# A causal head-wise convolution ahead of a channel mix: all of it on the path with x as the stationary operand, output with channels on partitions, and no intermediate in DRAM

## The chip, the cores and the metric

The kernel runs on one core of a Trainium2 chip. A core has a TensorE (PE) for matrix products, a VectorE (DVE), a ScalarE (ACT) and a GpSimd (POOL) for everything elementwise, a SyncE (SP) that issues DMAs here, and 16 DMA engines. The metric is the device time of one execution in microseconds (us), taken as the median of several runs. TensorE takes a *stationary* operand, loaded by an instruction of its own (LDWEIGHTS), and streams a *moving* operand past it. The array can be addressed in smaller tiles: a row "64*128" in the profile is a stationary operand of 64 partitions by 128 columns, "128*32" one of 128 partitions by 32 columns, "32*32" one of 32 by 32. Results go to PSUM[...].

## What is computed

```python
def _attn_ref(x, weight):                       # x (8, 4160, 192), weight (8, 7)
    w = softmax(weight, axis=-1)
    x_pad = concat([zeros((B, 6, D)), x], axis=1)
    idx = np.arange(S)[:, None] + np.arange(K)[None, :]
    x_unf = x_pad[:, idx, :].reshape(B, S, K, H, group)      # group = 24 channels
    return np.einsum('hk,bskhg->bshg', w, x_unf).reshape(B, S, D)

def _moe_ref(x, mu_k, mu_r, w_k, w_v, w_r):     # x is the result above; d_ff = 1024
    x_prev = x shifted by one token
    xk = mu_k * x + (1.0 - mu_k) * x_prev
    xr = mu_r * x + (1.0 - mu_r) * x_prev
    k = np.maximum(xk @ w_k, 0.0)
    v = k * k @ w_v
    r = 1.0 / (1.0 + np.exp(-(xr @ w_r)))
    return r * v
```

Each of the 8 heads filters its 24 channels along the tokens with 7 taps; then the channel mix follows.

## The kernel before

**Tiling.** The 8 batches are taken in four pairs. A pair's 4160 tokens are cut into steps of 512. The convolution's result for a pair lies in `yT`, with channels on partitions: three chunks of 64 channels, the two batches of the pair on the lower and upper 64 partitions. From it VectorE makes `diff`, `xk` and `xr` of each step.

**Bundles.** Work is issued in an order written out by hand, in 65 *bundles*. A steady bundle (`bundle_rest`) has four slots of the k product (`k_mm`, 6 matmuls of 64x512 each), four `k_relu` on ScalarE, four `k_square` on VectorE, a quad of the r product with its sigmoid (`r`, `r_out`), and a quad of the v product in two halves (`v_rows`, 32 matmuls of 64x192 each) with the multiplication `v_out`, whose result SyncE writes to `out`. The order on TensorE is k0, k1, k2, r, v half 0, k3, then the convolution's units of this bundle, then v half 1. Tables (`early`, `mix_a`, `mix_b`, `mix_c`, `late`, `xt`) say what else is issued in which bundle and at which point; `xt[b]` is the list of convolution units of bundle b. Every PSUM tile has two banks and comes from `ring`, which holds four of them; a tile is free again when the last reader is through, so a late reader on ScalarE or VectorE can hold up TensorE.

**The convolution, four ways.** `toe` holds for each head a banded matrix of taps, 128 by 128. A block is 120 new tokens with 6 of halo.

- `conv_t` (groups 0 to 2, the first 11 blocks of pair 0): x is stationary, 128 tokens by up to 32 channels; the band of a head (128x120) moves. The output has channels on partitions, and one copy (`to_yT`) per chunk puts it into `yT`. A strip of 32 channels meets two heads, so each strip takes two matmuls, the second of 24, 16 or 8 columns over the first. A block of one chunk is 8 matmuls: 2 batches, 2 strips, 2 heads.
- `conv_mm` (group 3): the band is stationary in 64x128 tiles, x moves, tokens come out on partitions; `conv_out` casts on ScalarE into `y`, and `tr` transposes on TensorE.
- `conv_tiles` (groups 4 and 5): 64x64 tiles of the band, x moves; ScalarE casts into `y` (`cast_tiles`); `y_write` sends `y` to a DRAM buffer, and `y_read` brings it back with a transposing DMA into `yT`, both from SyncE's queue.
- `conv_sparse` (groups 6 to 11, that is pairs 1 to 3): 32x32 tiles of the band, 26 new tokens of each 32 rows; 32 matmuls of 32x240, two PSUM tiles and four casts in a unit; then through DRAM as above. There are 24 such units, one in a bundle, in bundles 7 to about 51.

x comes from DRAM by DMAs that GpSimd issues and that cast to bf16 (`load_x`); small memsets on VectorE (L111, L123) order them behind the reuse of their buffers.

Of the kernel before, what the change touches and what calls it, by code (L numbers as in the profile page):

```python
# [14 lines left out]
def kernel(  # L15
# [23 lines left out]
    GB = 10  # L39
    HB = 56  # L40
    TB = 26
    TG = 20
    NROW = -(-S // (2 * HB)) * 2 * HB
# [9 lines left out]
    const = ctx.enter_context(tc.tile_pool(name="const", bufs=1))  # L53
    two = ctx.enter_context(tc.tile_pool(name="two", bufs=2))
# [3 lines left out]
    dram = ctx.enter_context(tc.tile_pool(name="dram", bufs=1, space=bass.MemoryType.DRAM))  # L58
# [32 lines left out]
    for p in range(NPAIR):  # L91
        base = 0
        for nb, s, on_pe in (
            ((3, 0, True), (4, 1, True), (4, 2, True), (5, 3, True), (10, 4, False), (10, 6, False))
            if p == 0
            else ((TG, 0, None), (TG, 4, None))
        ):
            if on_pe is None:
                base = min(base, S - nb * 4 * TB)
            groups.append((p, base, nb, first_bundle[first_step[p] + s], on_pe))  # L100
            base += nb * (4 * TB if on_pe is None else BLK if on_pe else 2 * HB)
        assert S <= base <= NROW
    sparse = {g for g, grp in enumerate(groups) if grp[4] is None}
    ends = [nxt[1] if nxt[0] == grp[0] else S for grp, nxt in zip(groups, groups[1:] + [(NPAIR,)])]


    xbs, homes = {}, {}

    def tie_x(g, s):

        nc.vector.memset(xbs[g][0:1, 1, s, 0:2], 0.0)  # L111

    def x_tile(g):
        p, base, nb, _, on_pe = groups[g]
        first = g if g in sparse else 4 * (g > 3)
        if g == first:
            homes[g] = two.tile([P, TG, 2, D], BF16, tag="xb", name="xb")
        n0 = sum(grp[2] for grp in groups[first:g])
        xb = homes[first][:, n0 : n0 + nb, :, :]
        xbs[g] = xb  # L120
        if g > 4:

            nc.vector.memset(xb[0:1, 0, 0, 0:2], 0.0)  # L123
        if base == 0 and g > 0:
            nc.gpsimd.memset(xb[0:32, 0, :, :], 0.0)  # L125
        if on_pe is False and base + 2 * nb * HB > S:
            n0 = nb - (base + 2 * nb * HB - S) // HB - 1
            nc.gpsimd.memset(xb[Q:P, n0:nb, :, :], 0.0)

    def load_x(g, batches=range(2)):  # L130
        p, base, nb, _, on_pe = groups[g]
        xb = xbs[g]
        if on_pe:
            parts, step, rows = ((0, base),), BLK, P
        elif g in sparse:
            parts, step, rows = [(32 * i, base + i * nb * TB) for i in range(4)], TB, 32
        else:
            parts, step, rows = ((0, base), (Q, base + nb * HB)), HB, Q
        for s in batches:
            b = 2 * p + s  # L140
            for q0, start in parts:
                lo, hi = 0, nb
                t0 = start - HALO
                if t0 < 0:
                    lo = 1
                    nc.gpsimd.dma_start(out=xb[HALO:rows, 0, s, :], in_=x[b, 0 : rows - HALO, :])
                while t0 + (hi - 1) * step + HALO + step > S:
                    hi -= 1
                    r0 = t0 + hi * step
                    if r0 + HALO < S:  # L150
                        nc.gpsimd.dma_start(out=xb[q0 : q0 + S - r0, hi, s, :], in_=x[b, r0:S, :])
                nc.gpsimd.dma_start(  # L152
                    out=xb[q0 : q0 + rows, lo:hi, s, :],
                    in_=bass.AP(
                        tensor=x.tensor,
                        offset=x.offset + (b * S + t0 + lo * step) * D,
                        ap=[[D, rows], [step * D, hi - lo], [1, D]],
                    ),
                )
# [140 lines left out]
    ys, yTs, y_drams = {}, {}, {}  # L300
    conv_ps = {}

    def conv_tiles(g, c):

        nb = groups[g][2]
        if c == 0:
            ys[g] = two.tile([P, GB, 2 * D], BF16, tag="y", name="y")
        ps = ring.tile([P, 2, BANK], FP32, tag="k", name="ps_c")
        conv_ps[g, c] = ps
        m = nb // 2  # L310
        banks = ps[:, :, 0 : m * 4 * G].rearrange("p i (m s c) -> p i m s c", m=m, s=2)
        for k in range(2):
            h = 2 * c + k
            for i in range(2):
                q = slice(i * Q, (i + 1) * Q)
                for j in range(2):
                    nc.tensor.matmul(  # L317
                        out=banks[j * Q : (j + 1) * Q, i, :, :, k * G : (k + 1) * G],
                        lhsT=toe[q, h, q],
                        rhs=xbs[g][q, j * m : (j + 1) * m, :, h * G : (h + 1) * G],  # L320
                        start=True,
                        stop=True,
                    )

    def conv_tiles_out(g, c):

        cast_tiles(ys[g], conv_ps.pop((g, c)), groups[g][2] // 2, c)

    def cast_tiles(y, ps, m, c):

        c0, c1 = 2 * c * G, 2 * (c + 1) * G
        cuts = [c0] + [a for a in range(Q, D, Q) if c0 < a < c1] + [c1]
        for a, b in zip(cuts, cuts[1:]):
            d = a // Q * 2 * Q + a % Q
            nc.scalar.copy(  # L335
                out=bass.AP(
                    tensor=y.tensor,
                    offset=y.offset + d,
                    ap=[y.ap[0], [m * 2 * D, 2], [2 * D, m], [Q, 2], [1, b - a]],
                ),  # L340
                in_=bass.AP(
                    tensor=ps.tensor,
                    offset=ps.offset + a - c0,
                    ap=[ps.ap[0], [BANK, 2], [4 * G, m], [2 * G, 2], [1, b - a]],
                ),
            )

    def conv_sparse(g, c):

        nb = groups[g][2]  # L350
        m = nb // 4
        if c == 0:
            ys[g] = [two.tile([P, GB, 2 * D], BF16, tag="y", name="y") for _ in range(2)]
        tiles = [ring.tile([P, 2, BANK], FP32, tag="k", name="ps_c") for _ in range(2)]
        xb = xbs[g].rearrange("p (m j) s c -> p j m s c", j=4)
        for k in range(2):
            h = 2 * c + k
            for i in range(4):
                q = slice(32 * i, 32 * i + 32)
                banks = tiles[i // 2][:, i % 2, 0 : m * 4 * G].rearrange("p (m s c) -> p m s c", m=m, s=2)  # L360
                for j in range(4):
                    nc.tensor.matmul(  # L362
                        out=banks[32 * j : 32 * j + 32, :, :, k * G : (k + 1) * G],
                        lhsT=toe[q, h, q],
                        rhs=xb[q, j, :, :, h * G : (h + 1) * G],
                        start=True,
                        stop=True,
                    )
        for y, ps in zip(ys[g], tiles):
            cast_tiles(y, ps, m, c)  # L370

    def conv_units(g):

        return [((0, 1), (6, 7)), ((2, 3), (4, 5))]

    def conv_mm(g, c, half):

        nb = groups[g][2]
        if half == 0:
            if c == 0:  # L380
                ys[g] = two.tile([P, GB, 2 * D], BF16, tag="y", name="y")
            conv_ps[g, c] = ring.tile([P, 2, BANK], FP32, tag="k", name="ps_c")
        unit = conv_units(g)[c]
        last = len(unit[0]) - 1
        banks = conv_ps[g, c][:, :, 0 : nb * 2 * G * (last + 1)].rearrange("p i (n s c) -> p i n s c", n=nb, s=2)
        for k in range(last + 1):
            for i in range(2):
                q = slice(i * Q, (i + 1) * Q)
                bank = (i + half) % 2
                h = unit[bank][k]  # L390
                nc.tensor.matmul(
                    out=banks[:, bank, :, :, k * G : (k + 1) * G],
                    lhsT=toe[q, h, :],
                    rhs=xbs[g][q, :nb, :, h * G : (h + 1) * G],
                    start=half == 0 and k == 0,
                    stop=half == 1 and k == last,
                )
        if half == 0:
            nc.scalar.clobber_nop([nc.scalar.lower_ap(conv_ps[g, c])])
# [54 lines left out]


    def y_write(g):
        p, base, nb, _, _ = groups[g]
        if base == 0:
            new_yT(p)
        if g in sparse:  # L460
# [604 lines left out]
```

## Time and profile before

Three runs took 410.29, 411.07 and 411.44 us. The profiled execution took 411.28 us; its span, from the first to the last instruction, is 409.5 us, so 1.78 us lie around it. The granted TensorE clock was 1.00.

| stretch of the span (us) | PE busy | DVE busy | ACT busy | POOL busy | mean of DMA share | GB/s |
|---|---|---|---|---|---|---|
| 0 to 12 | 9.51 | 7.42 | 7.41 | 10.38 | 0.97 | 152 |
| 12 to 28.8 | 15.47 | 15.23 | 15.76 | 7.02 | 1.59 | 190 |
| 28.8 to 57.93 | 28.95 | 27.66 | 27.37 | 6.59 | 1.24 | 217 |
| 57.93 to 312 | 253.56 | 235.45 | 231.65 | 32.23 | 0.90 | 175 |
| 312 to 409.5 | 93.74 | 84.65 | 72.46 | 0.61 | 0.39 | 108 |

The stretches are: start, ramp, the `conv_tiles` units, the `conv_sparse` units (57.93 is the first of them, 312 lies just behind the last), and the rest, in which no convolution is left. Busy times are in us; the DMA share is the busy time of the 16 DMA engines over the stretch and can exceed 1 where transfers overlap on one engine. To read it: compare each engine's busy time with the length of its stretch, then see which engine has no gap left.

### The profile page before, as it was taken

Reading aid. Unit: us, or ns where it says so; the run is one execution under the profiler, and the core shown is the slowest. Engines: PE = TensorE matmul, PEld = TensorE weight load, DVE = VectorE, ACT = ScalarE, POOL = GpSimd, SP = SyncE. Lnnn points to the kernel's source line nnn. Section 1 sums busy time; section 2 is a strip of 40 time slices with the busy share of each in tenths; the row PEclk is TensorE's granted clock in tenths of the full one; section 3 lists DMA queues with packets and bytes.
Section 4 is the critical chain, followed back from the end, with each engine's and each line's share of the span. In section 5 each row is a group of like instructions: output and inputs, shape, how many; then the busy total and the mean of one; then the engine's idle time right before and its main releaser. Section 6 shows DMA issues by size and latency. Waiting matters only on the chain.

```text
span 409.5 us, 17547 instructions
## 1 busy us (share of the span) xinstructions
PE 401.2 (98%) x7736; PEld 302.2 (74%) x7736; DVE 370.4 (90%) x672; ACT 354.6 (87%) x426; POOL 56.8 (14%) x91
## 2 busy tenths in 40 slices
PE   8899999999999999999999999999999999999996
PEld 5567777777877767777776777777777778777795
DVE  5999898988999989999999999999999899999973
ACT  6899989989888989988898998889899878877781
POOL 8622202200230202004020022000000000000000
PEclk9999999999999999999999999999999999999999
DMA  9999999997399998789995996977623856221223
GB/s 148 188 201 207 197 204 192 213 249 179 90 203 264 193 193 134 158 212 178 205 141 151 236 170 132 171 176 206 121 91 89 209 135 157 80 71 48 80 80 115
DMA packets 138955, 66.23 MB, mean 162 GB/s; under 512 B 89356, under 2 KB 138880, under 8 KB 138880
## 3 DMA queue, kind: packets, MB, share of 16 engines
q1 hardware_dynamic: 95536, 48.20, 46.9%
q0 software_dynamic: 42544, 16.36, 34.8%
q8 instruction: 60, 0.98, 0.9%
q10 hardware_dynamic: 800, 0.57, 0.5%
q14 instruction: 15, 0.12, 0.1%
HBM read 33.29 MB, written 36.86 MB: 171 GB/s over the span
## 4 chain that ended last, share of the span: by engine, by line
PE 92%; DMA 4%; POOL 1%; DVE 1%; ACT 1%; issue 1%; POOLq 0%; DVEq 0%
PE ps_v L679 41%; PE ps_k L591 39%; PE ps_r L648 8%; PE ps_c L362 2%; DMA xb<-in_x_dram 2%; DMA wk<-in_moe_w_k_dram 2%; PE ps_v L631 1%; ACT k_sb L603 1%; PE ps_c L317 0%; POOL wk L224 0%; POOL xb L152 0%; DVE k L617 0%; DVE yT L421 0%; DVE o_sb L695 0%; POOL tap L258 0%
## 5 line engine op out<-in xcount | busy, mean ns | idle before, releaser
L603 ACT ACTIVATE k_sb<-ps_k 128x1024 bf16<-128x1024 f32 x260 | 253.3, 1038 | 34.9 <-PE ps_k L591 33.8
L617 DVE TENSOR_TENSOR k<-k_sb 128x1024 bf16<-128x1024 bf16 x260 | 173.6, 688 | 26.1 <-ACT k_sb L603 25.8
L591 PE MATMUL ps_k<-xk,wk 64*128 64x512 bf16 (+1 forms) x1632 | 192.0, 367 | 1.5 <-DMA wk<-in_moe_w_k_dram 1.3
L679 PE MATMUL ps_v<-wv,k 64*128 64x192 bf16 x4032 | 188.5, 243 | 0.5 <-DMA wv<-in_moe_w_v_dram 0.5
L679 PEld LDWEIGHTS <-k 64*128 64x128 bf16 x4032 | 168.2, 94 | 13.1 <-issue 4.6
L591 PEld LDWEIGHTS <-wk 64*128 64x128 bf16 x1632 | 83.6, 94 | 56.9 <-issue 2.0
L695 DVE TENSOR_TENSOR o_sb<-ps_v,r_sb 128x768 f32<-128x768 f32 x64 | 60.9, 951 | 2.6 <-issue 2.4
L152 POOL DMA_DIRECT2D xb<-in_x_dram x62 | 43.5, 708 | 131.8 <-DVE xb L111 59.8
L659 ACT ACTIVATE r_sb<-ps_r 128x768 bf16<-128x768 f32 x65 | 53.4, 824 | 7.9 <-PE ps_v L679 5.7
L335 ACT CAST y<-ps_c 128x960 bf16<-128x960 f32 (+2 forms) x84 | 52.6, 708 | 0.0
L648 PEld LDWEIGHTS <-xr 64*128 64x128 bf16 x780 | 35.0, 94 | 14.8 <-issue 1.0
L648 PE MATMUL ps_r<-wr,xr 64*128 64x192 bf16 x780 | 43.4, 243 | 0.3 <-issue 0.3
L565 DVE TENSOR_SCALAR xr<-d,mu 128x512 bf16<-128x512 bf16 (+1 forms) x102 | 35.2, 349 | 0.0
L565 DVE TENSOR_SCALAR xk<-d,mu 128x512 bf16<-128x512 bf16 (+1 forms) x99 | 32.5, 358 | 0.1
L534 DVE TENSOR_TENSOR d<-yT 128x1536 bf16<-128x1536 bf16 (+4 forms) x36 | 31.2, 867 | 1.2 <-ACT yT L421 1.1
L571 DVE TENSOR_TENSOR xr<-xr,yT 128x1536 bf16<-128x1536 bf16 (+1 forms) x33 | 31.1, 941 | 1.1
L571 DVE TENSOR_TENSOR xk<-xk,yT 128x1536 bf16<-128x1536 bf16 (+3 forms) x33 | 30.5, 925 | 0.1
L518 POOL COPY y_tail<-yT 128x195 bf16<-128x195 bf16 x4 | 2.8, 690 | 89.1 <-DMA yT<-y_dram 89.1
L362 PEld LDWEIGHTS <-toe 32*32 32x32 bf16 x768 | 4.9, 87 | 10.2 <-issue 8.7
L362 PE MATMUL ps_c<-xb,toe 32*32 32x240 bf16 x768 | 10.7, 267 | 0.0
L125 POOL MEMSET xb<- 32x384 bf16 x3 | 1.2, 407 | 67.1 <-DVE xb L123 67.1
L411 PE MATMUL ps_t<-toe,xb 128*32 128x120 bf16 (+3 forms) x264 | 5.4, 234 | 0.3 <-ACT yT L421 0.2
(60 smaller groups left out, 61.8 us busy)
## 6 DMA issues: line engine op xcount, KB each, us to landing
out_dram<-o_sb SPq DMA_DIRECT2D x128, 192.0 KB
xb<-in_x_dram POOLq DMA_DIRECT2D x52, 240.0 KB, 8.1
y_dram<-y SPq DMA_DIRECT2D x48, 195.0 KB
y_dram<-y SPq DMA_DIRECT2D x8, 210.0 KB
xb<-in_x_dram POOLq DMA_DIRECT2D x6, 228.0 KB, 4.7
xb<-in_x_dram POOLq DMA_DIRECT2D x4, 192.0 KB, 6.5
wk<-in_moe_w_k_dram POOLq DMA_DIRECT2D x4, 192.0 KB, 6.2
wv<-in_moe_w_v_dram POOLq DMA_DIRECT2D x1, 384.0 KB, 10.1
```

The source lines that it names most:

```text
L152: nc.gpsimd.dma_start(out=xb[q0 : q0 + rows, lo:hi, s, :], in_=bass.AP(tensor=x.tensor, offset=x.offset + (b * S + t0 + lo * step) * D, ap ...
L335: nc.scalar.copy(out=bass.AP(tensor=y.tensor, offset=y.offset + d, ap=[y.ap[0], [m * 2 * D, 2], [2 * D, m], [Q, 2], [1, b - a]],), in_=bas ...
L534: nc.vector.tensor_tensor(out=shaped(s, diffs[s][:, cs, :L]), in0=y_of(s, cs, 1), in1=y_of(s, cs, 0), op=ALU.subtract)
L565: nc.vector.tensor_scalar(out=t[:, c, :L], in0=diffs[s][:, c, :L], scalar1=mu[:, i, c : c + 1], scalar2=None, op0=ALU.mult)
L571: nc.vector.tensor_tensor(out=o, in0=o, in1=y_of(s, sl, 0), op=ALU.add)
L591: nc.tensor.matmul(out=ps[:, i, f * L : (f + 1) * L], lhsT=wk[r, c, fs], rhs=xk[r, c, :L], start=c == 0 and f == 0, stop=c == NC - 1 and f ...
L603: nc.scalar.activation(out=k_sb, in_=ps.rearrange("p a b -> p (a b)"), func=AF.Relu)
L617: nc.vector.tensor_tensor(out=o, in0=i, in1=i, op=ALU.mult)
L648: nc.tensor.matmul(out=ps[:, i, k * D : (k + 1) * D], lhsT=xr[q, c, ts], rhs=wr[q, c, :], start=c == 0, stop=c == NC - 1,)
L659: nc.scalar.activation(out=r_sbs[s, j], in_=r_ps.pop((s, j))[:, :, 0 : 2 * D], func=AF.Sigmoid)
L679: nc.tensor.matmul(out=v_ps[s, j][:, bank, k * D : (k + 1) * D], lhsT=k2s[s][q, f, t * P : (t + 1) * P], rhs=wv[q, f, :], start=half == 0 ...
L695: nc.vector.tensor_tensor(out=o_sb.rearrange("p (b t) d -> p b (t d)", b=2), in0=v_ps.pop((s, j)), in1=r_sbs.pop((s, j)), op=ALU.mult,)
```

## The change

All four ways become `conv_t`. The groups are now of 4 blocks (3 at one end of each pair), 36 in all, 9 per pair; 3 are done in the first two bundles as before, and the other 33 give 99 units of one group and one chunk. Units go in their order, two to a bundle, into bundles 1 to 50 (the last has one). `conv_pair` takes one two-bank tile of the ring, writes one unit into each bank, and copies each into `yT`: on ScalarE, except the second unit of an odd bundle, which VectorE copies. It stands where the units stood: after k3 in bundle 1, between v half 0 and k2 in bundle 2, and between k3 and v half 1 in the others. `conv_mm`, `conv_tiles`, `conv_sparse`, their casts, `tr`, `y_write`, `y_read` and the DRAM buffers are gone. x is loaded by groups of 4 blocks into eight small buffers, five bundles ahead of use, two DMAs of 128 rows in each group and a few for the ends.

```diff
-        for nb, s, on_pe in (
-            ((3, 0, True), (4, 1, True), (4, 2, True), (5, 3, True), (10, 4, False), (10, 6, False))
-            if p == 0
-            else ((TG, 0, None), (TG, 4, None))
-        ):
...
+        for nb in (3,) + 8 * (4,) if p == 0 else 8 * (4,) + (3,):
+            groups.append((p, base, nb))
+            base += nb * BLK
...
+        xb = eight.tile([P, 4, 2, D], BF16, tag="xb", name="xb")[:, :nb, :, :]
...
+    def to_yT(g, c, o, copy):
+        p, base, nb = groups[g]
+        n = min(nb * BLK, S - base)
+        copy(out=yTs[p][:, c, YC + base : YC + base + n], in_=o[:, 0:n])
+
+    def conv_pair(b):
+
+        units = xt.get(b, [])
+        if not units:
+            return
+        o = ring.tile([P, 2, BANK], FP32, tag="k", name="ps_t")
+        for k, (g, c) in enumerate(units):
+            if groups[g][1] == 0 and c == 0:
+                new_yT(groups[g][0])
+            conv_t(g, c, o[:, k, :], range(groups[g][2]))
+        for k, (g, c) in enumerate(units):
+            to_yT(g, c, o[:, k, :], nc.vector.tensor_copy if k and b % 2 else nc.scalar.copy)
...
+    units = [(g, c) for g in range(3, len(groups)) for c in range(NC)]
+    for n, u in enumerate(units):
+        xt.setdefault(1 + n // 2, []).append(u)
+    for g in range(5, len(groups)):
+        b = max(1, 1 + (units.index((g, 0))) // 2 - 5)
+        at(mix_a if b == 1 else early, b, x_tile, g)
+        at(mix_a if b == 1 else early, b, load_x, g)
...
         run(mix_a, b)
-        conv_half(xt[b][0], 0)
         k_relu(ns[3])
-        conv_half(xt[b][0], 1)
         k_square(ns[1])
         run(mix_b, b)
-        conv_mm(*xt[b][1], 0)
-        conv_mm(*xt[b][1], 1)
+        conv_pair(b)
...
-            tr(3, 0)
-            tr(3, 1)
...
-            for u in xt[b - 1]:
-                conv_tiles(*u)
-                conv_tiles_out(*u)
...
-        for u in units:
-            if u[0] in sparse:
-                conv_sparse(*u)
-            else:
-                conv_tiles(*u)
-                conv_tiles_out(*u)
+        conv_pair(b)
         v_rows(*quad, 1)
...
         v_rows(*quad, 0)
-        conv_out(*xt[b - 1][1], nc.scalar.copy)
+        conv_pair(b)
```

More of the change, by code (lines that the diff above doesn't have):

```diff
@@ L38 @@
     BLK = 120
[L39 to L43, printed above, removed]
     BANK = 512
@@ L53 @@
     const = ctx.enter_context(tc.tile_pool(name="const", bufs=1))
+    eight = ctx.enter_context(tc.tile_pool(name="eight", bufs=8))
     two = ctx.enter_context(tc.tile_pool(name="two", bufs=2))
@@ L57 @@
     ring = ctx.enter_context(tc.tile_pool(name="ring", bufs=4, space=bass.MemoryType.PSUM))
-    dram = ctx.enter_context(tc.tile_pool(name="dram", bufs=1, space=bass.MemoryType.DRAM))
     steps = []
@@ L92 @@
         base = 0
-        for nb, s, on_pe in (
-            ((3, 0, True), (4, 1, True), (4, 2, True), (5, 3, True), (10, 4, False), (10, 6, False))
-            if p == 0
-            else ((TG, 0, None), (TG, 4, None))
-        ):
[L98 to L111, printed above, removed]
-    def x_tile(g):
[L114 to L119, printed above, removed]
+        for nb in (3,) + 8 * (4,) if p == 0 else 8 * (4,) + (3,):
+            groups.append((p, base, nb))
+            base += nb * BLK
@@ L120, in x_tile @@
+        assert S <= base
+    xbs = {}
+    def x_tile(g):
+        p, base, nb = groups[g]
+        xb = eight.tile([P, 4, 2, D], BF16, tag="xb", name="xb")[:, :nb, :, :]
         xbs[g] = xb
         if g > 4:
-            nc.vector.memset(xb[0:1, 0, 0, 0:2], 0.0)
+            nc.vector.memset(xb[0:1, 1, 0, 0:2], 0.0)
         if base == 0 and g > 0:
             nc.gpsimd.memset(xb[0:32, 0, :, :], 0.0)
-        if on_pe is False and base + 2 * nb * HB > S:
-            n0 = nb - (base + 2 * nb * HB - S) // HB - 1
-            nc.gpsimd.memset(xb[Q:P, n0:nb, :, :], 0.0)
@@ L130, in load_x @@
-    def load_x(g, batches=range(2)):
-        p, base, nb, _, on_pe = groups[g]
-        xb = xbs[g]
[L133 to L136, printed above, removed]
-        else:
-            parts, step, rows = ((0, base), (Q, base + nb * HB)), HB, Q
-        for s in batches:
-            b = 2 * p + s
[L141 to L159, printed above, removed]
@@ new lines, in x_tile, with load_x @@
+        if base + nb * BLK > S:
+            nc.gpsimd.memset(xb[Q:P, nb - 1, :, :], 0.0)
+    def load_x(g):
+        p, base, nb = groups[g]
+        xb = xbs[g]
+        for s in range(2):
+            b = 2 * p + s
+            lo, hi = 0, nb
+            t0 = base - HALO
+            if t0 < 0:
+                lo = 1
+                nc.gpsimd.dma_start(out=xb[HALO:P, 0, s, :], in_=x[b, 0 : P - HALO, :])
+            while t0 + (hi - 1) * BLK + P > S:
+                hi -= 1
+                r0 = t0 + hi * BLK
+                if r0 + HALO < S:
+                    nc.gpsimd.dma_start(out=xb[0 : S - r0, hi, s, :], in_=x[b, r0:S, :])
+            nc.gpsimd.dma_start(
+                out=xb[:, lo:hi, s, :],
+                in_=bass.AP(
+                    tensor=x.tensor,
+                    offset=x.offset + (b * S + t0 + lo * BLK) * D,
+                    ap=[[D, P], [BLK * D, hi - lo], [1, D]],
+                ),
+            )
@@ L299, in make_toe @@
             )
[L300 to L399, printed above, removed]
+    yTs = {}
@@ L417, in conv_t @@
                         )
-    def to_yT(g, c, o, b0, b1, copy):
-        c0 = YC + groups[g][1] + b0 * BLK
-        copy(out=yTs[0][:, c, c0 : c0 + (b1 - b0) * BLK], in_=o[:, 0 : (b1 - b0) * BLK])
-    def conv_out(g, c, copy):
-        nb = groups[g][2]
-        unit = conv_units(g)[c]
-        w = G * len(unit[0])
-        ps = conv_ps.pop((g, c))[:BLK, :, :]
-        y = ys[g][:BLK, :, :]
-        parts = []
-        for hs in unit:
-            c0, c1 = hs[0] * G, (hs[-1] + 1) * G
-            cuts = [c0] + [a for a in range(Q, D, Q) if c0 < a < c1] + [c1]
-            parts.append(sorted((b - a, a - c0, a // Q * 2 * Q + a % Q) for a, b in zip(cuts, cuts[1:])))
-        for (n, s0, d0), (m, s1, d1) in zip(*parts):
-            assert n == m and d1 > d0
-            copy(
-                out=bass.AP(
-                    tensor=y.tensor,
-                    offset=y.offset + d0,
-                    ap=[y.ap[0], [d1 - d0, 2], [2 * D, nb], [Q, 2], [1, n]],
-                ),
-                in_=bass.AP(
-                    tensor=ps.tensor,
-                    offset=ps.offset + s0,
-                    ap=[ps.ap[0], [BANK + s1 - s0, 2], [2 * w, nb], [w, 2], [1, n]],
-                ),
-            )
@@ new lines, in to_yT @@
+    def to_yT(g, c, o, copy):
+        p, base, nb = groups[g]
+        n = min(nb * BLK, S - base)
[11 more added lines that the diff above has]
+            to_yT(g, c, o[:, k, :], nc.vector.tensor_copy if k and b % 2 else nc.scalar.copy)
@@ L450, in new_yT @@
     def new_yT(p):
         yTs[p] = two.tile([P, 3, -(-(YC + S) // 16) * 16], BF16, tag="yT", name="yT")
-        y_drams[p] = dram.tile([NROW, 2 * D], BF16, tag=f"y{p % 2}", name="y_dram")
         nc.vector.memset(yTs[p][:, :, 0:YC], 0.0)
[L456 to L460, printed above, removed]
-            m = nb // 4
-            for half in range(2):
-                for j in range(4):
-                    nc.sync.dma_start(
-                        out=bass.AP(
-                            tensor=y_drams[p].tensor,
-                            offset=y_drams[p].offset + (base + (2 * half * nb + j) * TB) * 2 * D,
-                            ap=[[2 * D, TB], [4 * TB * 2 * D, 2 * m], [1, 2 * D]],
-                        ),
-                        in_=ys[g][half][32 * j : 32 * j + TB, :, :],
-                    )
-            return
-        m = nb // 2
-        for i in range(2):
-            for j in range(2):
-                r0 = base + (i * nb + j * m) * HB
-                nc.sync.dma_start(
-                    out=y_drams[p][r0 : r0 + m * HB, :].rearrange("(n t) c -> t n c", t=HB),
-                    in_=ys[g][j * Q : j * Q + HB, i * m : (i + 1) * m, :],
-                )
@@ L482, in y_read @@
-    def y_read(g, part=slice(0, 1), of=1):
-        p, base = groups[g][:2]
-        n = (ends[g] - base) // of
-        r0, r1 = base + part.start * n, base + part.stop * n
-        nc.sync.dma_start_transpose(
-            out=yTs[p][:, :, YC + r0 : YC + r1], in_=y_drams[p][r0:r1, :]
-        )
-    def tr(g, j):
-        p, base, nb, _, _ = groups[g]
-        ps = ring.tile([P, 2, 2 * BANK], BF16, tag="k", name="ps_t")
-        todo = range(4 * j, min(nb, 4 * j + 4))
-        view = ps[:, :, 0 : 6 * BLK].rearrange("p b (c i t) -> p b c i t", c=3, i=2)
-        for i0 in todo[::2]:
-            for c in range(3):
-                for i in range(i0, min(nb, i0 + 2)):
-                    nc.tensor.transpose(
-                        out=view[:, (i - 4 * j) // 2, c, i % 2, :],
-                        in_=ys[g][:BLK, i, c * P : (c + 1) * P],
-                        identity=ident[:BLK, :BLK],
-                    )
-        for i in todo[::2]:
-            n = min(2, nb - i)
-            c0 = YC + base + i * BLK
-            nc.vector.tensor_copy(
-                out=yTs[p][:, :, c0 : c0 + n * BLK].rearrange("p c (n t) -> p c n t", n=n),
-                in_=view[:, (i - 4 * j) // 2, :, :n, :],
-            )
@@ L734, in at @@
         table.setdefault(b, []).append((fn, a))
-    def conv_half(unit, half):
-        if unit is not None:
-            conv_mm(*unit, half)
-            if half == 1:
-                conv_out(*unit, nc.scalar.copy)
-    for g, (p, base, nb, fb, on_pe) in enumerate(groups):
-        if g < 3:
-            continue
-        if p == 0:
-            xs = {3: [1, 1], 4: [2, 2, 3, 3], 5: [4, 4, 5, 5]}[g]
-        else:
-            xs = {6: [7, 8, 9, 10], 7: [12, 13, 15, 17]}.get(g, [fb - 13, fb - 11, fb - 9, fb - 7])
-        for i, b in enumerate(xs):
-            xt.setdefault(b, []).append((g, i))
-        if not on_pe:
-            at(late, xs[-1], y_write, g)
-        if g in sparse:
-            at(late, max(fb - 5, xs[-1] + 2), y_read, g, slice(0, 1), 2)
-            at(late, fb - 2, y_read, g, slice(1, 2), 2)
-            b, b1 = {6: (3, 5), 7: (9, 10), 8: (16, 17)}.get(g, (fb - 19, fb - 16))
-            at(early, b, x_tile, g)
-            at(early, b, load_x, g, (0,))
-            table = mix_c if g == 6 else early
-            at(table, b1, tie_x, g, 1)
-            at(table, b1, load_x, g, (1,))
-            continue
-        if not on_pe:
-            if g == 4:
-                at(mix_c, 4, y_read, g, slice(0, 1), 2)
-                at(late, 4, y_read, g, slice(1, 2), 2)
-            else:
-                at(late, 6, y_read, g)
-        if g > 4:
-            at(mix_a, 1, x_tile, g)
-            at(mix_a, 1, load_x, g)
+    units = [(g, c) for g in range(3, len(groups)) for c in range(NC)]
[5 more added lines that the diff above has]
+        at(mix_a if b == 1 else early, b, load_x, g)
     for s, (p, t0, L, n0, ns) in enumerate(steps):
@@ L877, in bundle_first @@
                 turn_mu()
-            to_yT(g, c, o, 0, groups[g][2], nc.scalar.copy)
+            to_yT(g, c, o, nc.scalar.copy)
             if g == 0:
@@ L909, in bundle_second @@
         conv_t(g, 0, outs[0], range(4))
-        to_yT(g, 0, outs[0], 0, 4, dve_)
+        to_yT(g, 0, outs[0], dve_)
         k_relu(ns[1])
         conv_t(g, 1, outs[1], range(4))
-        to_yT(g, 1, outs[1], 0, 4, dve_)
+        to_yT(g, 1, outs[1], dve_)
         k_mm(ns[2])
@@ L916, in bundle_second @@
         conv_t(g, 2, outs[2], range(4))
-        to_yT(g, 2, outs[2], 0, 4, act_)
+        to_yT(g, 2, outs[2], act_)
         k_mm(ns[3])
@@ L973, in bundle_rest @@
         run(rs, b, slice(1, None))
-        for u in units:
-            if u[0] in sparse:
-                conv_sparse(*u)
-            else:
-                conv_tiles(*u)
-                conv_tiles_out(*u)
+        conv_pair(b)
         v_rows(*quad, 1)
```

## The prediction, made before the changed kernel ran

> **What bounds the kernel now.** I read the busy times first, then the chain of waits, then TensorE's timeline. From the page:
>
> ```profile
> PE 401.2 (98%) x7736; PEld 302.2 (74%) x7736; DVE 370.4 (90%) x672; ACT 354.6 (87%) x426; POOL 56.8 (14%) x91
> PE 92%; DMA 4%; POOL 1%; DVE 1%; ACT 1%; issue 1%; POOLq 0%; DVEq 0%
> ```
>
> TensorE has work in 401.2 of 409.5 us, and 92% of the chain that ended last is TensorE. Only 8.3 us of it are idle: 3.8 before 28.8 us (start and ramp), 3.8 after 312 (mostly the end), by the busy times of these stretches. So whatever adds TensorE time adds it to the end, and relief elsewhere can return at most part of 8.3 us. The same is seen in the timeline of TensorE (start, length, instruction, count), two bundles in the middle:
>
> ```profile
> 161.61 0.83 PE L591 MATMUL ps_k<-xk,wk 64*128 64x512 bf16 x6
> 162.26 1.50 PE L679 MATMUL ps_v<-wv,k 64*128 64x192 bf16 x32
> ...
> 167.34 0.83 PE L591 MATMUL ps_k<-xk,wk 64*128 64x512 bf16 x6
> 168.10 0.42 PE L362 MATMUL ps_c<-xb,toe 32*32 32x240 bf16 x32
> 168.46 1.50 PE L679 MATMUL ps_v<-wv,k 64*128 64x192 bf16 x32
> ...
> 173.54 0.81 PE L591 MATMUL ps_k<-xk,wk 64*128 64x512 bf16 x6
> ```
>
> From k3 to the next k3 a bundle without a convolution takes 167.34 - 161.61 = 5.73 us, one with a `conv_sparse` unit 173.54 - 167.34 = 6.20. After 312 us, with no convolution left and the DMA share down from 0.90 to 0.39, bundles still take 5.73 to 5.74. So traffic doesn't slow TensorE here: **removing the DRAM way is worth nothing by itself**. Only TensorE's time for the convolution matters.
>
> **What the change removes from TensorE.**
> - 24 `conv_sparse` units. Five bundles with one (from 155.38, 167.34, 179.27, 191.19 and 203.17 us) take 6.20 to 6.24, mean 6.22; less 5.735, that is 0.487 each: 11.7 us.
> - Four pairs of `conv_tiles` units. One bundle takes 38.81 to 45.18 = 6.37, so 0.64; three at that, and the first, from 28.83 to 29.81, 0.98: 2.9 us.
> - `conv_mm`, from 18.74 to 20.09: 1.35. `tr`, from the end of k1 (27.83) to 28.83: 1.0.
>
> Sum: **17.0 us**.
>
> **What it adds.** The path itself runs in the trace of before, at the start, in the second bundle (PEld is the weight load):
>
> ```profile
> 15.73 0.85 PEld L411 LDWEIGHTS <-xb 128*32 128x32 bf16 x64 [0.42 <-issue]
> 15.73 1.02 PE L411 MATMUL ps_t<-toe,xb 128*32 128x120 bf16 x64
> ...
> 16.68 0.44 PEld L591 LDWEIGHTS <-wk 64*128 64x128 bf16 x6
> 16.80 0.82 PE L591 MATMUL ps_k<-xk,wk 64*128 64x512 bf16 x6
> 17.55 0.43 PEld L411 LDWEIGHTS <-xb 128*32 128x32 bf16 x32 [0.42 <-issue]
> 17.55 0.60 PE L411 MATMUL ps_t<-toe,xb 128*32 128x120 bf16 x32
> 18.09 0.82 PE L591 MATMUL ps_k<-xk,wk 64*128 64x512 bf16 x6
> ```
>
> The first 64 matmuls are just what `conv_pair` issues. One matmul lasts 216 ns (the median of L411), mostly pipeline; so starts are (1.02 - 0.216)/63 = 12.8 ns apart, and in the 32 (0.60 - 0.216)/31 = 12.4. The array passes four column tiles at once.
>
> The price of a pair: a gap from k3 to the first matmul, 17.55 - (16.80 + 0.64) = 0.11 (six k matmuls take 0.64: 161.61 to 162.26); 63 starts at 12.8 ns, 0.81; the last stream, a quarter-rate of four, 0.05; and the gap to the next tile shape. That gap is 0.22 and 0.11 in front of k above, and 0.10 between `conv_sparse` and v, the neighbour that `conv_pair` has in 48 bundles. With 0.13: **1.10 us**. Bounds: 1.03 (12.5 ns and both gaps 0.10 to 0.12) and 1.18 (16.80 - 15.73, plus 0.11).
>
> Number: 33 groups x 3 chunks = 99 units = 49.5 pairs. Nine units have 3 blocks: 72 matmuls less, 0.9 us. So 49.5 x 1.10 - 0.9 = **53.6 us** (50.1 to 57.5).
>
> Net 53.6 - 17.0 = +36.6 us (33 to 41).
>
> **Rule against row.** The Trainium skill, "TensorE: Matmul & The Clock Gate", section on packing small matmuls, says weight loads overlap running matmuls only where the row group differs. `conv_t` uses all 128 rows every time, so by that rule no load would hide: with the page's P/1.2, 27 ns for 32 columns, 3096 matmuls would pay some 84 us in loads beside their streaming, and the kernel would take about 530 us (an estimate from that page). The same page puts a floor of 25 ns between matmul starts: 49.5 x (64 x 0.025 + 0.29) = 94, a kernel of about 488. The rows above show 64 loads in 0.85 us beside 64 matmuls in 1.02, at 12.8 ns: column tiles do overlap here. I take the row.
>
> **ScalarE.** The casts of `y` go (L335 25.7 + 19.9 + 12.5, L437 2.1: 60.2 us). 74 copies come, at this price:
>
> ```profile
> L421 ACT CAST yT<-ps_t 128x480 bf16<-128x480 f32 x4 | 2.2, 557 | 0.5 <-PE ps_t L411 0.3
> L421 DVE CAST yT<-ps_t 128x480 bf16<-128x480 f32 x2 | 1.2, 648 | 0.0
> ```
>
> 74 x 0.557 = 41. ScalarE gets 19 us lighter; it isn't the bound, so nothing comes back.
>
> **VectorE.** 25 copies x 0.648 = 16.2, less 1.3 of `tr`'s copies: 385 us of some 446. In an odd bundle it has squares 2.7, `v_out` 0.95, mixing 2.6, copy 0.65: 6.9, beside TensorE's 5.73 + 1.10 = 6.83; in an even one 6.1. Over two bundles 13.0 against 13.7, so it fits. The local wait is `v_out`, which must free its PSUM tile before the next r. In the odd bundle of 209.41 it runs 212.32 to 213.27 and the next r starts at 213.33. With the change v half 1 and that r come 1.10 later, and `v_out`, behind one copy, at most 0.65 later: no wait. If that cover goes, I set 0.1 to 0.5 us on 25 odd bundles, 2 to 12 us.
>
> **PSUM ring.** `conv_pair` takes one tile where `conv_sparse` took two. Its copies end about 1.3 us (even) after the pair, v half 1 and two k slots (1.32 + 1.28) come before that tile is wanted: no wait.
>
> **Queues.** SyncE loses 56 writes and 15 transposing reads and keeps the output: not on the path. GpSimd issues x about a dozen times more, at 0.71 us, 9 us on an engine that is 14% busy; loads go out five bundles (34 us) ahead against 8.1 us to landing. The one tight spot is bundle 2, which now wants group 4 (before, its first use was at 28.83). Its two DMAs stand behind `wv`, whose landing ended TensorE's wait at 22.60; 0.39 MB (2 x 128 x 4 x 192 values of 2 bytes) at the 190 GB/s moved from 12 to 28.8 us is 2.1 us more, 24.7, less 0.5 because group 3 is one block smaller. The pair starts about 24.0 with group 3, 24.4 with group 4. So between no wait and 1 us; I take none, as the two numbers meet. The x tie memsets on VectorE wait for a convolution six bundles back: nothing. POOL's `keep_tail` no longer waits for a transposed read: hidden before, hidden after.
>
> **Sum.** 409.5 + 36.6 = 446.1 of span, plus the 1.78 around it: **448 us**. The profiled execution (411.28) stands 0.2 above the median (411.07), so no correction is made.
>
> **Rivals.**
> 1. *A dearer stream.* In the first bundle the same instructions ran slower: 24 in 0.79 us (25 ns) at 5.94, 48 in 1.14 (19.7 ns) at 6.86. For it: same shapes. Against: it is the start, and from 8.2 us on the loads go at 12 ns. At 19.7 a pair costs 1.53: 49.5 x 1.53 - 1.4 - 17.0 = +57, **469 us**.
> 2. *VectorE or the ring sets odd bundles.* For it: 6.9 against 6.83. Against: the slack of even bundles and `v_out` above. +36.6 + 2 to 12: **450 to 460 us**.
> 3. *The other side: the convolution's matmuls cost nothing.* If they filled array time that k and v leave open, only the removal would count: 409.5 - 17.0 + 1.8 = **394 us**. Place: between k3 and v half 1; it decides once a pair costs less than 17.0/49.5 = 0.34 us. Against: 64 matmuls took 1.07 us start to start, during which no k or v matmul starts, and streaming alone is 0.8.
> 4. *It doesn't do what it says.* The diff has no DRAM tile left and the unit count follows from the groups; I see no room for it.
>
> **Chances.** Forecast with its bounds (442 to 453) 0.80; rival 2 beyond that 0.09; rival 1 0.08; rival 3 0.02; a cancelling mix near 411, 0.01. A measurement of this kernel can tell 0.3% (1.2 us) from no change. Faster 0.02, same 0.01, slower 0.97. The range is 440 to 461: the forecast's bounds, 2 us below for a smoother start, and rival 2 above; rival 1 stays outside.
>
> **What would show it.** TensorE again at 97% or more of a longer span; L411 with 3360 matmuls, 64 in about 1.0 us; bundles of about 6.8 us up to bundle 50 and 5.73 after; DMA share well lower without a gain; ScalarE about 336 us, VectorE about 385. Wrong would be: TensorE idle by more than 15 us, waits of k, r or `ps_t` on VectorE, the first group-4 matmul waiting for xb, or a pair under 1.03 or over 1.18 us.

## The result and the profile after

Three runs of the changed kernel took 449.47, 449.75 and 451.12 us: median 449.75 against 411.07 before, a ratio of 1.095 (95% interval 1.091 to 1.100). Forecast were 448 us and a range of 440 to 461. The profiled execution took 451.12, with a span of 449.4. From its page: instructions of the engines, shares of the chain of waits, the group of `conv_t` on TensorE and its weight loads, the two kinds of copies, and the DMA queue named "instruction":

```profile
PE 436.4 (97%) x9968; PEld 332.3 (74%) x9969; DVE 388.4 (86%) x712; ACT 339.8 (76%) x413; POOL 71.5 (16%) x111
PE 94%; issue 2%; DMA 2%; POOL 1%; ACT 0%; DVE 0%; POOLq 0%; DVEq 0%
L283 PEld LDWEIGHTS <-xb 128*32 128x32 bf16 (+3 forms) x3360 | 45.7, 94 | 28.4 <-issue 27.6
L283 PE MATMUL ps_t<-toe,xb 128*32 128x120 bf16 (+3 forms) x3360 | 56.3, 219 | 5.5 <-issue 5.1
L294 ACT CAST yT<-ps_t 128x480 bf16<-128x480 f32 (+3 forms) x81 | 41.5, 544 | 6.3 <-PE ps_t L283 5.8
L294 DVE CAST yT<-ps_t 128x480 bf16<-128x480 f32 (+2 forms) x27 | 17.3, 643 | 26.3 <-ACT yT L294 25.3
q8 instruction: 78, 1.28, 1.2%
```

TensorE is still the bound, with 35 us more work (436.4 us against 401.2), and the two engines that copy are below it. New is the end of the fourth line: TensorE stood idle for 5.5 us ahead of `conv_t`'s matmuls, 5.1 of them "issue", that is, waiting for nothing that the profile names.

A steady bundle, in TensorE's timeline (start, length, instruction, count):

```profile
179.79 0.81 PE L391 MATMUL ps_k<-xk,wk 64*128 64x512 bf16 x6
180.53 1.02 PE L283 MATMUL ps_t<-toe,xb 128*32 128x120 bf16 x64
181.48 1.49 PE L479 MATMUL ps_v<-wv,k 64*128 64x192 bf16 x32
...
186.57 0.81 PE L391 MATMUL ps_k<-xk,wk 64*128 64x512 bf16 x6
```

From k3 to k3 it takes 6.78 us (the median over the steady bundles is 6.785), 1.05 more than the 5.735 without a convolution: 0.10 from the end of k3 (179.79 + 0.64) to the burst, 0.95 from the burst to v. The burst has the length that it had in the trace of before, 1.02.

The ramp, in the same view:

```profile
15.63 0.49 PE L283 MATMUL ps_t<-toe,xb 128*32 128x120 bf16 x21
17.10 0.75 PE L283 MATMUL ps_t<-toe,xb 128*16 128x120 bf16 x43 [0.98 <-issue]
17.78 0.82 PE L391 MATMUL ps_k<-xk,wk 64*128 64x512 bf16 x6
18.53 0.60 PE L283 MATMUL ps_t<-toe,xb 128*32 128x120 bf16 x32
19.07 0.82 PE L391 MATMUL ps_k<-xk,wk 64*128 64x512 bf16 x6
19.82 0.75 PE L283 MATMUL ps_t<-toe,xb 128*32 128x120 bf16 x41
23.30 0.49 PE L283 MATMUL ps_t<-toe,xb 128*32 128x120 bf16 x23 [2.73 <-issue]
...
26.94 0.81 PE L283 MATMUL ps_t<-toe,xb 128*32 128x120 bf16 x48
29.15 0.40 PE L283 MATMUL ps_t<-toe,xb 128*32 128x120 bf16 x16 [1.39 <-issue]
```

Three times a burst stops in the middle, for 0.98, 2.73 and 1.39 us. Is it x that comes late? No: the second stop comes after 41 of 64 matmuls that all read group 3, whose two DMAs had landed at 17.08 and 17.83; the third comes after two blocks of group 4, landed at 21.73 and 23.01; and the matmul that ends a stop waits for no semaphore. But count what TensorE issues between the first two stops: 43 + 6 + 32 + 6 + 41 = 128 matmuls, each with a weight load, which is **256 instructions**. The page's queue q8 moved 78 packets, of 16 KB each, for a program of some 20,000 instructions on TensorE: 256 to a packet. Those packets begin at 14.60, 20.92 and 26.89 us, take 0.9 us, and each stop ends 1.3 to 1.6 us after the end of one of them. The Trainium skill, "Runtime: NRT & Kernel Launch", section on instruction fetch mechanics, says that an engine's instructions come in blocks of 256 by DMA, the next block while the current one runs, and calls the cost "mostly hidden". Here the blocks are seen; the cost, in the ramp, isn't hidden.

The count holds beyond these three. Take the traces of the changed kernel and of all the runs below, eleven in all, and count TensorE's instructions up to each wait of over 0.2 us behind 14 us that the profile names "issue". There are 37 such waits; all lie a multiple of 256 instructions apart (within 3, as single records are missing), and TensorE goes on 1.05 to 1.62 us after the end of a packet. The result's one longer wait behind the ramp, 0.70 us at 162 us, which the profile puts down to "DVE k", stands at such a place too.

So two theories stood for the difference between forecast and result. **Instruction fetch**: the next block is asked for at about the time when the last one begins (inferred; the trace shows the packet, not the request), stands in the DMA queues behind x and the weights, and is late when TensorE uses up a block too fast. **TensorE's own time only**, the forecast: stalls of that kind don't exist, or x is late.

### The profile page after: what moved, and what is told of

The parts are those of the page before. It is cut to its first block, busy times and chain, and to the rows that moved or that the text cites. A ratio compares the mean times of both kernels' runs of the same rounds, so it can differ in the third digit from the quotient of the medians.

```text
span 449.4 us, 21973 instructions
## 1 busy us (share of the span) xinstructions
PE 436.4 (97%) x9968; PEld 332.3 (74%) x9969; DVE 388.4 (86%) x712; ACT 339.8 (76%) x413; POOL 71.5 (16%) x111
## 4 chain that ended last, share of the span: by engine, by line
PE 94%; issue 2%; DMA 2%; POOL 1%; ACT 0%; DVE 0%; POOLq 0%; DVEq 0%
PE ps_v L479 38%; PE ps_k L391 37%; PE ps_t L283 11%; PE ps_r L448 7%; DMA wk<-in_moe_w_k_dram 2%; PE ps_v L431 1%; POOL wk L195 0%; POOL xb L123 0%; ACT k_sb L403 0%; DVE k L417 0%; ACT yT L294 0%; POOL tap L229 0%; DVE o_sb L515 0%; POOL band L257 0%; POOL band L254 0%
## 5 line engine op out<-in xcount | busy, mean ns | idle before, releaser
L479 PEld LDWEIGHTS <-k 64*128 64x128 bf16 x4032 | 166.2, 94 | 9.1 <-issue 0.9
L391 PEld LDWEIGHTS <-wk 64*128 64x128 bf16 x1632 | 80.7, 94 | 58.5 <-DMA wk<-in_moe_w_k_dram 1.1
L123 POOL DMA_DIRECT2D xb<-in_x_dram x70 | 52.4, 752 | 239.9 <-PE ps_v L479 83.9
L495 DVE TENSOR_TENSOR o_sb<-ps_v,r_sb 128x768 f32<-128x768 f32 x64 | 60.9, 952 | 8.4 <-PE ps_v L479 5.6
L283 PEld LDWEIGHTS <-xb 128*32 128x32 bf16 (+3 forms) x3360 | 45.7, 94 | 28.4 <-issue 27.6
L283 PE MATMUL ps_t<-toe,xb 128*32 128x120 bf16 (+3 forms) x3360 | 56.3, 219 | 5.5 <-issue 5.1
L294 ACT CAST yT<-ps_t 128x480 bf16<-128x480 f32 (+3 forms) x81 | 41.5, 544 | 6.3 <-PE ps_t L283 5.8
L294 DVE CAST yT<-ps_t 128x480 bf16<-128x480 f32 (+2 forms) x27 | 17.3, 643 | 26.3 <-ACT yT L294 25.3
L365 DVE TENSOR_SCALAR xr<-d,mu 128x512 bf16<-128x512 bf16 (+1 forms) x102 | 36.9, 366 | 0.0
L431 PE MATMUL ps_v<-wv,k 128*128 128x192 bf16 x64 | 5.5, 247 | 0.0
```

What stands on the lines that cost most here:

```text
L123: nc.gpsimd.dma_start(out=xb[:, lo:hi, s, :], in_=bass.AP(tensor=x.tensor, offset=x.offset + (b * S + t0 + lo * BLK) * D, ap=[[D, P], [BLK ...
L283: nc.tensor.matmul(out=o[p0 : p0 + m, n * BLK : (n + 1) * BLK], lhsT=xbs[g][:, i, s, c0 : c0 + m], rhs=toe[:, h, 0:BLK], start=True, stop= ...
L294: copy(out=yTs[p][:, c, YC + base : YC + base + n], in_=o[:, 0:n])
L365: nc.vector.tensor_scalar(out=t[:, c, :L], in0=diffs[s][:, c, :L], scalar1=mu[:, i, c : c + 1], scalar2=None, op0=ALU.mult)
L391: nc.tensor.matmul(out=ps[:, i, f * L : (f + 1) * L], lhsT=wk[r, c, fs], rhs=xk[r, c, :L], start=c == 0 and f == 0, stop=c == NC - 1 and f ...
L479: nc.tensor.matmul(out=v_ps[s, j][:, bank, k * D : (k + 1) * D], lhsT=k2s[s][q, f, t * P : (t + 1) * P], rhs=wv[q, f, :], start=half == 0 ...
```

## Experiments

Each was timed beside the kernel before on the same chip, whose medians were 411.25 to 411.42 us. The changed kernel was run again beside two of them:

> The changed kernel itself once more, on the same chip as the next two, to compare them. 449 to 451 us by both theories; by instruction fetch the stalls of the first 30 us vary from run to run, and their sum goes with the span.

It took 449.83 us (ratio 1.094, 1.090 to 1.098). In its profiled execution, the slowest of its six at 453.47, the first stop is absent, the second is 2.12, the third 2.49, and there is one of 2.07 at 161 us, at the instruction where the result's trace has its 0.70. The stops in the ramp come at the same instructions as before (after 41 of 64, after 48 of 64); their lengths differ.

**Late loads.** x of groups 5 and later is issued two bundles ahead.

```diff
-        b = max(1, 1 + (units.index((g, 0))) // 2 - 5)
-        at(mix_a if b == 1 else early, b, x_tile, g)
-        at(mix_a if b == 1 else early, b, load_x, g)
+        b = 1 + units.index((g, 0)) // 2 - 2
+        at(late, b, x_tile, g)
+        at(late, b, load_x, g)
```

> The changed kernel with x of groups 5 and later issued two bundles ahead, at the bundle's end, instead of five. In the profile of the changed kernel TensorE stands still three times in the first 30 us, 0.98, 2.73 and 1.39 us, each in the middle of a burst of ps_t. Instruction fetch: the third one goes or shrinks below 0.5 (the fetch asked for at 23.3 us finds the queues nearly empty after the landing of group 4 at 23.0), the first two stay; 447.5 to 449.5 us. Theory 'x comes late' (the prediction's bundle-2 wait): the third stays at 1.4 or grows, and later loads add waits: 450 us or more.

448.10 us (ratio 1.088, 1.083 to 1.093). Repeated beside the changed kernel:

> The run with late loads once more, beside the changed kernel on the same chip. Instruction fetch: 1 to 2.5 us below the changed kernel. Theory 'x comes late': the same or above it.

447.79 us (1.089, 1.085 to 1.093) against 449.83: 2.0 us less, though the two intervals overlap. The repeated run's profile, its fastest execution, shows what went. TensorE's timeline:

```profile
18.32 0.75 PE L283 MATMUL ps_t<-toe,xb 128*32 128x120 bf16 x41
21.41 0.50 PE L283 MATMUL ps_t<-toe,xb 128*32 128x120 bf16 x23 [2.34 <-issue]
...
25.06 1.02 PE L283 MATMUL ps_t<-toe,xb 128*32 128x120 bf16 x64
```

The second stop is there, after 41 matmuls; the burst of bundle 2, which stopped after 48, now runs through. Loads that come *later* took a stall away, so x was not what it waited for. (The first stop, 0.98, was expected to stay and is missing in both runs; of the eleven traces only the result's has it.)

**No load of wv.** As above, and wv is set to zero without a DMA, which takes 0.39 MB out of the queue ahead of the second stop. The output is then zero; only the time counts.

```diff
-        nc.gpsimd.dma_start(out=wv, in_=moe_w_v.rearrange("(f p) d -> p f d", p=P))
+        nc.vector.memset(wv, 0.0)
```

> As the run with late loads, and the load of wv is left out (wv is zero, so the output is zero). Instruction fetch: 0.39 MB less stands in the queues when the second block of the ramp is asked for at about 17 us, so the stall of 2.73 us falls to 1.5 or less; the three stalls together from 5.1 us to 2.5 or less, and bundle 3 begins 2.5 us or more before 32.1 us. Theory 'x comes late': group 3, which this burst reads, had been asked for before wv, so the stall of 2.73 us stays.

447.41 us (1.086, 1.081 to 1.090). The timeline of its profiled execution, the fastest of four at 444.98:

```profile
18.52 0.75 PE L283 MATMUL ps_t<-toe,xb 128*32 128x120 bf16 x41
20.36 0.50 PE L283 MATMUL ps_t<-toe,xb 128*32 128x120 bf16 x23 [1.08 <-issue]
...
24.00 1.02 PE L283 MATMUL ps_t<-toe,xb 128*32 128x120 bf16 x64
```

The second stop is 1.08, after the same 41 matmuls, although the burst reads nothing of wv. With late loads alone it was 2.29 and 2.34, and in all nine other traces with every matmul 1.84 to 2.73. Bundle 3 begins at 27.58, against 28.64 and 30.35 with late loads alone and 32.10 in the result. The median, 0.4 to 0.7 us below late loads alone, is not clear of noise. The evidence is one trace, then, and it says that the length of a stop follows the load on the DMA queues, and its place the count of instructions.

**The traffic put back.** A round trip through DRAM of the removed size, which nobody reads (66.0 MB are moved in all, 66.2 before the change and 42.2 after it):

```diff
+        nc.sync.dma_start(
+            out=drams[p][base : base + nb * BLK, :].rearrange("(n t) c -> t n c", t=BLK),
+            in_=xbs[g][0:BLK, :, :, :].rearrange("t n s d -> t n (s d)"),
+        )
...
+        nc.sync.dma_start_transpose(out=back[:, :, 0:n], in_=drams[p][base : base + n, :])
```

> The changed kernel plus a round trip through DRAM of the size that was removed: for each group of 4 blocks SyncE writes 0.37 MB to DRAM and reads it back with a transposing DMA into a tile that nobody reads (33 groups, 12 MB each way). Theory 'TensorE's own time only', as the prediction had it (traffic doesn't slow TensorE): 449 to 451 us, no new idle time of TensorE, with the DMA share back near 0.8. Theory 'instruction fetch': TensorE's program comes in blocks of 256 instructions by DMA, one block ahead; with conv_t a block lasts only 4.0 to 5.3 us in the steady part (5.5 to 6.4 before), so longer waits of the fetch behind other traffic show as idle TensorE inside the bursts of ps_t or elsewhere at block ends: 452 to 462 us.

454.28 us (1.104, 1.099 to 1.109). Repeated:

> The run with the round trip through DRAM once more, beside the changed kernel on the same chip. Instruction fetch: 2 us or more above the changed kernel, with stalls of 1 us and more at ends of 256-instruction blocks behind 36 us. TensorE's own time only: within 1 us.

454.09 us (1.103, 1.100 to 1.106) against 449.83 (1.090 to 1.098) on the same chip: 4.3 us more, and the intervals don't meet. One of the stops, in TensorE's timeline of the repeated run:

```profile
117.30 0.92 PE L284 MATMUL ps_t<-toe,xb 128*32 128x120 bf16 x55
119.94 0.32 PE L284 MATMUL ps_t<-toe,xb 128*8 128x120 bf16 x9 [1.73 <-issue]
```

Behind 36 us TensorE is idle for 4.0 us in this execution (3.8 in the first run's), against 1.0 in the result's. The steady bundle stays at 6.785 us in both, so the traffic doesn't slow the matmuls themselves. From bundle 3 to the end both traces take 420.2 us, 2.9 more than the result's 417.3, and the added idle time, 2.8 and 3.0 us, accounts for it. The rest of the 4.3 is not located. (The repeat of the changed kernel was profiled in its slowest execution, with 2.5 us idle and a stretch at half clock, on which the last section has more, and doesn't show the difference.) So traffic is not free beside `conv_t`. Between 36 and 350 us a packet started, in the median, 1.2 to 1.3 us after the first matmul of the block before with the traffic, 0.5 to 0.65 without; in all four traces it was 4.1 at most, and some packets started up to 1.3 us ahead of that matmul. A block lasted as little as 4.1 us in the changed kernel and here, 5.5 in the kernel before, where packets started as much as 5.0 us late and no stop behind 36 us passed 0.3.

**Half of the matmuls.** From group 3 on the second matmul of each strip is left out, so some channels get the taps of the wrong head; only the time counts.

```diff
-            for first_piece in (True, False):
+            for first_piece in (True, False) if g < 3 else (True,):
```

> The changed kernel without the second matmul of each strip from group 3 on (the channels that belong to the lower head get the upper head's taps). 1548 of 3096 matmuls fall away. Theory 'streaming at 12.8 ns each plus a fixed 0.23 us per pair': 19.8 us less, and up to 5 us of startup stalls: 425 to 430 us; a pair falls from 1.05 to 0.64 us. Rival 'the price is mostly fixed per pair (changes of tile shape, first weights)': 440 us or more, a pair at 0.85 or more.

431.25 us (1.048, 1.044 to 1.051), 1.3 us above the expected range. Its timeline, TensorE in two bundles and two rows of VectorE (`v_out` is L495):

```profile
199.70 0.81 PE L391 MATMUL ps_k<-xk,wk 64*128 64x512 bf16 x6
200.44 0.60 PE L283 MATMUL ps_t<-toe,xb 128*32 128x120 bf16 x32
200.97 1.50 PE L479 MATMUL ps_v<-wv,k 64*128 64x192 bf16 x32
202.06 0.66 DVE L294 CAST yT<-ps_t 128x480 bf16<-128x480 f32 x1 [0.86 <-ACT yT L294]
202.30 2.11 PE L391 MATMUL ps_k<-xk,wk 64*128 64x512 bf16 x18
203.50 0.95 DVE L495 TENSOR_TENSOR o_sb<-ps_v,r_sb 128x768 f32<-128x768 f32 x1
204.51 0.67 PE L448 MATMUL ps_r<-wr,xr 64*128 64x192 bf16 x12
...
206.32 0.83 PE L391 MATMUL ps_k<-xk,wk 64*128 64x512 bf16 x6
...
208.94 2.11 PE L391 MATMUL ps_k<-xk,wk 64*128 64x512 bf16 x18
210.88 0.66 PE L448 MATMUL ps_r<-wr,xr 64*128 64x192 bf16 x12
...
212.70 0.81 PE L391 MATMUL ps_k<-xk,wk 64*128 64x512 bf16 x6
```

The second bundle takes 6.38, so a pair costs 0.645 (6.38 less the 5.735 of a bundle without one): the streaming price holds, and the rival of a fixed price falls. The first takes 6.62. There r starts at 204.51, 2.21 after k0, where the other bundle has 1.94. The cause is `v_out`, which runs on VectorE until 204.45 behind a copy; in the two longest of these waits, 0.38 and 0.34 us, the profile names it. With 0.24 us in every second bundle, 24 bundles, that is 5.8 us, nearly all of the excess over the lower end. The wait of rival 2 is real, then; it shows in this run, whose bundles are 0.4 us shorter.

**Four units in every second bundle.**

```diff
-        xt.setdefault(1 + n // 2, []).append(u)
+        xt.setdefault(1 + n // 2 if n < 4 else 3 + (n - 4) // 4 * 2, []).append(u)
```

> The changed kernel with four units in every second bundle from bundle 3 on, as two pairs back to back, instead of two in each. Theory 'fixed 0.23 us per visit to the tile shape': 24 visits fewer, 5.5 us less: 444 us, and a quad costs 1.87 us. Theory 'instruction fetch': a burst is now 256 instructions, a whole block, in 1.7 us, less than a fetch takes (1 us and more of waiting and packet, and some 1.4 after it); TensorE stands still in many bursts: 446 to 465 us.

456.18 us (1.107, 1.102 to 1.113), 6.4 more, not 5.5 less. What TensorE waited for (group, releaser: us in all, times, longest):

```profile
PE ps_v L481 <- issue: 6.4, 6, 1.7
PE ps_t L283 <- issue: 6.2, 6, 2.1
```

A burst that runs through costs 1.91 us (105.42 + 0.64 to 107.97), near the expected 1.87, so the visits are saved as expected. But the stops named "issue" rise to 12.6 us, 4.1 of them in the ramp; behind 36 us TensorE stands idle for 9.4, 0.7 of them r waiting for `v_out`. A burst is one block of instructions in 1.8 us, and its stop comes inside or just behind it. This run can't share the rest out: all these bundles are odd, so VectorE had twice the copies behind each burst.

**All second units copied by VectorE.**

```diff
-            to_yT(g, c, o[:, k, :], nc.vector.tensor_copy if k and b % 2 else nc.scalar.copy)
+            to_yT(g, c, o[:, k, :], nc.vector.tensor_copy if k else nc.scalar.copy)
```

> The changed kernel with the second unit of every bundle copied by VectorE, not of odd bundles alone: 24 copies, some 16 us, move from ScalarE to VectorE, which then has about 404 us. Theory 'TensorE alone sets the time': 449 to 451 us. Rival 2 of the prediction (VectorE or the ring sets the bundle): 455 us or more.

451.21 us (1.095, 1.091 to 1.099), steady bundles 6.785 as in the changed kernel. VectorE, at 397.5 us, has nine more than there. One k product waits 0.76 us for VectorE, in bundle 3, and TensorE's time is otherwise unmoved. VectorE doesn't set the changed kernel's time.

**The two units apart.** One ahead of k2, one in the old place.

```diff
         run(mix_c, b)
+        conv_pair(b, slice(0, 1))
         k_mm(ns[2])
...
-        conv_pair(b)
+        conv_pair(b, slice(1, 2))
         v_rows(*quad, 1)
```

> The changed kernel with the two units of a bundle apart from bundle 3 on: one ahead of k2, one in the old place, each with a PSUM tile of its own. Theory 'fixed 0.23 us per visit': 48 visits more, 11 us: 461 us (a little less where shorter bursts help the instruction fetch). Rival 'the price goes with the matmuls alone': 449 to 451 us.

458.65 us (1.113, 1.109 to 1.117): 8.9 more. TensorE's timeline, one bundle from k3 to k3:

```profile
155.42 0.81 PE L391 MATMUL ps_k<-xk,wk 64*128 64x512 bf16 x6
156.16 0.60 PE L283 MATMUL ps_t<-toe,xb 128*32 128x120 bf16 x32
156.69 1.49 PE L479 MATMUL ps_v<-wv,k 64*128 64x192 bf16 x32
158.02 1.46 PE L391 MATMUL ps_k<-xk,wk 64*128 64x512 bf16 x12
159.41 0.60 PE L283 MATMUL ps_t<-toe,xb 128*32 128x120 bf16 x32
...
162.42 0.81 PE L391 MATMUL ps_k<-xk,wk 64*128 64x512 bf16 x6
```

A steady bundle takes 7.004, that is 0.22 for the second visit, 10.5 us over 48 bundles; behind 36 us no stop is left, and the burst of bundle 2 stops for 0.28. Of those 10.5 us 1.6 came back; in its trace the stops are 3.2 us shorter than in the result's (2.9 against 6.1).

## Why the prediction came out right, and where its sum was off

- *What bounds the kernel*: right. TensorE is busy for 97% of the span; the removal of the DRAM way gave nothing back.
- *Price of a pair*: 1.10 was said, with bounds 1.03 and 1.18; 1.05 was measured. The gap to v is smaller than the 0.13 taken. The runs with half the matmuls and with units apart confirm its two parts: 32 matmuls fewer take 0.405 off (12.7 ns each), and a visit costs 0.22.
- *Sum from bundle 3 on.* Bundle 3's k0 started at 26.55 before and starts at 32.10 now, so the rest of the span grew from 382.95 to 417.30, by 34.35. By the forecast's terms, with 1.05: 47.5 pairs, 49.9, less 0.9 for the short units, less 15.6 removed (11.7 + 2.9 + 1.0), is 33.4; idle time behind 36 us adds 0.5 (1.0, against 0.5 before). The terms close to within 0.5.
- *The ramp* was mis-sized. The forecast set no wait, and up to 1 us for x of group 4 in bundle 2. The ramp grew by 5.55, of which 5.1 are the three stops; two pairs (2.1) less `conv_mm` (1.35) and less the wait of 0.55 at 22.60 add only 0.2. The step that failed is "Queues": it looked only at whether data lands in time, which it did, and not at TensorE's own program, which comes by DMA beside the data. The trace of before had a clue. That wait at 22.60, read as `wv` coming late, stands at the same place in the count of 256 and ends 1.51 us after the end of a packet; wv had landed at 22.29, so the trace leaves both causes open. For the whole span, 409.5 + 36.6 against 449.4 is 3.3 short: 6.1 of idle time, less 1.05 that the kernel before had, less 2.5 for the pair priced too high (0.05 x 49.5), is 2.6, and 0.7 is not accounted for. So it is in part luck that 448 came within 2 us: one error hid part of the other.
- *Traffic doesn't slow TensorE*: true of a steady bundle in both kernels, and true of the kernel before as a whole as far as its trace shows. In the changed one a round trip of the same size costs 4.3 us, of which the traces show 2.9 as stops at the ends of blocks. The reading came from a kernel whose blocks of instructions last longer (5.5 us at least, against 4.1).
- *Rule against row*: the row was right. 3360 weight loads with all 128 rows ran beside the matmuls, 64 in about a microsecond; by the skill's rule, as the prediction took it, the kernel would have taken some 530 us. (The same section also lets a load run ahead into a background weight buffer, which the prediction left out.)
- *ScalarE and VectorE*: forecast 336 and 385 us, measured 339.8 and 388.4. `v_out` keeps r waiting nowhere in the changed kernel.
- *Rivals*: 1 (19.7 ns) and 3 (matmuls hidden) are refuted by the steady bundle. 2 (VectorE) is refuted for this kernel; its wait appears in the run with half the matmuls, whose bundle is shorter. No version run here beats the kernel before.

## What to carry to other kernels

Where one engine fills the span, price a rewrite by that engine's instructions alone: the way through DRAM cost TensorE 0.49 us for a unit of two heads over half a pair of sequences, 3.9 us for a pair of batches, while x-stationary tiles cost 105/4/2 = 13.1 visits of 1.05 us, 13.8, for the same pair. Take the price from a burst of the same shape in the trace, and add the gaps where tile shapes change. And count instructions per microsecond: small matmuls can use up a block of 256 faster than the DMA queues deliver the next, above all while they are full.

## What the runs showed of the hardware

- TensorE's program comes in packets of 16 KB on a DMA queue of its own, one per 256 instructions. In the ramp, at a DMA share of 1.3 to 1.5, a packet of the changed kernel began 3.6 to 5.3 us after the block before it had begun, and TensorE went on 1.3 to 1.6 us after it had ended. Such a stop shows as "issue", often in the middle of a run of equal instructions, always at the end of a block, with a length that changes from run to run.
- A stop can cost more than its length. After a stop of 2.29 us, in the first run with late loads, the next twelve k matmuls took 2.67 us instead of 1.47, and the twelve of r 1.17 instead of 0.66: half the rate. After one of 2.34 in the repeated run they didn't. The granted clock (PEclk, last but two) tells them apart; busy time is the second number:

```profile
core 0: us, PE busy (x), PEclk, DMA share, GB/s
18.59:22.00 3.41, 1.12 (x66) 1.00 1.09 130
22.00:25.41 3.41, 3.41 (x26) 0.50 0.02 5
25.41:28.83 3.42, 3.42 (x116) 1.00 0.02 5
...
16.68:20.09 3.41, 2.39 (x83) 1.00 1.57 190
20.09:23.51 3.42, 2.10 (x45) 1.00 0.28 34
23.51:26.92 3.41, 3.41 (x116) 1.00 0.02 5
```

The first three rows are of the first run, the others of the repeated one. In all these traces the clock, once up, changes only at multiples of 3.41 us from its first rise. The stop of 2.29 lies within one such stretch; that of 2.34 is split between two, and so is the result's of 2.73. Four stretches had TensorE idle for 1.99 to 2.28 us, and each was followed by one stretch at 0.50 (first late loads, copies by VectorE, units apart, and the repeat of the changed kernel behind its stop at 161 us). None with 1.75 us or less was. Where between the two the line lies, no run shows.
